# Three of four attention units with scores by rows in place of two of three, and the order of a group's loads

## The chip, the cores and the metric

The kernel runs on one core of one Trainium2 chip. The metric is the device time in microseconds (us); the runs shown agree to the last digit, 1306.41 us. Smaller is better. All times of single instructions come from one execution recorded by the hardware profiler.

## What is computed

The reference is an adaptive layer norm around two blocks; only the first matters here.

```python
h = _layernorm(x, axis=-1) * (1 + ca) + sa
x = x + ga * _A_ref(h, A_k_cache, A_v_cache, A_wq, A_wo)     # attention
h = _layernorm(x, axis=-1) * (1 + cb) + sb
x = x + gb * _B_ref(h, B_w_in, B_w_sp, B_b_sp, B_w_out)      # gated MLP with a mix over positions

# _A_ref: 2048 queries, 2048 cached keys, 32 query heads of width 128 on 8 key/value heads
q = (x @ wq)...; scores = q k^T / sqrt(128); p = softmax(scores); o = p v; return o @ wo
```

Everything is bf16. Each of the 8 key/value heads serves a group of four query heads.

## The kernel before

**Units.** Attention is cut into `NU` = 128 units, numbered `u`: 8 groups (one key/value head each) by 16 tiles of 128 queries, all four query heads of the group in one unit. A unit has 8 slots. In iteration `it` the main loop issues, slot by slot, the scores of unit `it` (`qk`, L1016), the product with V of an earlier unit (`pv_part`, L1449), a quarter of the next block's Q projection (`fill`), and the output projection W_o of a still earlier unit (`wo_proj`, L1156). TensorE runs this in the order in which it is written; nothing is rescheduled.

**Two ways to compute a unit.** Both need 16 score matmuls of 128x512 and 8 exponentials of 128x1024 on ScalarE.

- *Without rows* (I call it a column unit): the scores come out transposed, keys on partitions (L1068), the exponential (L1075) is written straight into the unit's `pT` tile, and the product with V (L1124) takes 64 matmuls of 128x129, the extra column being the sum of the row. VectorE normalises (`onorm`, L1135/L1136), one DMA transpose of 128 KB on SP's queue turns `onorm` into `oT` (L1147), and the four heads of W_o add up in one PSUM bank, followed by one addition (L1168).
- *By rows* (a row unit): the scores have queries on partitions (L1031), the exponential (L1038) also sums its row, and writes into one of six row buffers `pn` (`win_sb` in three parts, `wmod_a`, and two tiles `pn`). When a head's two halves are done, one DMA transpose of 128x2048, 512 KB, on SP's queue carries it into the unit's `pT` tile (`turn_rows`, L1085, the DMA on L1088). The product with V (L1103) then takes 16 matmuls of 128x512 and gives `oT` directly. In exchange each head of W_o has its own bank and its own scaled addition on VectorE (L1174).

Each of the first matmuls with V of a row unit reads all four heads' columns of `pT`, so it needs all four transposes of the unit to have landed.

**Which unit is which, and when its product with V runs.** `by_rows` (L992) says yes for units from `TURN_A` = 5 up to `TURN_B` by a repeating pattern as long as `LAGS`, all of whose entries but the last are row units. `pv_at` (L997) puts the product with V as many units later as the entry says; column units have 1. With `LAGS = (2, 3, 1)` a period is: row (two units later), row (three later), column (one later). That makes 78 row units and 50 column units. `wo_at` is three units after that. Three homes for `pT` (`pT0`, `pT1`, and the tile `wsp`) are handed out in rotation.

**SP's queue** runs in the order in which it is written: the transposes of a row unit's heads one after another, the `onorm` transpose of a column unit behind the first row unit that follows it, and the loads. A column unit has no row transposes of its own.

**Loads.** Each group needs W_q, K (a DMA transpose from memory), V and W_o, 512 KB each, loaded during the group before (L1347 to L1362). Each is placed into slot 1 of the first column unit that comes at least `from_it` units after the start of the group before, one load in one column unit. All of it has two buffers. W_q of a group is first used four units before the group starts, K in its first unit, V one unit later, W_o four units later.

Of the kernel before, what the change touches and what calls it, by code (L numbers as in the profile page):

```python
# [575 lines left out]
def kernel(  # L576
# [19 lines left out]
    nc = tc.nc  # L596
# [13 lines left out]
    CT = 512 // P  # L610
# [107 lines left out]
    def load_wq(g, engine):  # L718
        wqs[g] = early.tile([P, NDT, REP * DH], BF16, name="wq_g")
        engine.dma_start(  # L720
            out=wqs[g][:], in_=wq_dram[:, :, g * REP * DH : (g + 1) * REP * DH]
        )

    def load_v(g):
        v1 = late.tile([P, NKT, DV], BF16, name="v1")
        nc.gpsimd.memset(v1[:, :, DH:DV], 1.0)
        if g > 0:
            nc.sync.dma_start(out=v1[:, :, 0:DH], in_=v_dram[:, g])
        else:
            nc.sync.dma_start(out=v1[:, 0 : NKT // 2, 0:DH], in_=v_rows)  # L730
            nc.sync.dma_start(
                out=v1[:, NKT // 2 : NKT, 0:DH], in_=v_dram[:, 0, NKT // 2 : NKT]
            )
        groups.setdefault(g, {})["v1"] = v1

    def load_wo(g, engine):
        wo_g = late.tile([P, REP, D], BF16, name="wo_g")
        engine.dma_start(out=wo_g[:], in_=wo_dram[:, g * REP : (g + 1) * REP, :])
        groups[g]["wo"] = wo_g

    def load_k(g):
        kT = early.tile([P, SK], BF16, name="kT")
        nc.sync.dma_start_transpose(out=kT[:], in_=A_k_cache[0, g])
        groups.setdefault(g, {})["kT"] = kT
# [240 lines left out]
    NU = HKV * NT  # L985


    TURN_A, TURN_B = CT + 1, NU - 6

    LAGS = (2, 3, 1)  # L990

    def by_rows(u):  # L992
        return TURN_A <= u < TURN_B and (u - TURN_A) % len(LAGS) < len(LAGS) - 1

    row_units = [u for u in range(NU) if by_rows(u)]

    def pv_at(u):  # L997
        return u + (LAGS[(u - TURN_A) % len(LAGS)] if by_rows(u) else 1)

# [13 lines left out]
    def at(it, slot, fn):  # L1013
        later.setdefault((it, slot), []).append(fn)
# [332 lines left out]
    for g in range(1, HKV):  # L1347
        it = (g - 1) * NT
        loads = (
            (0, lambda g=g: load_wq(g, nc.sync)),  # L1350
            (4, lambda g=g: load_v(g)),
            (6, lambda g=g: load_wo(g, nc.sync)),
            (8, lambda g=g: load_k(g)),
        )
        last = it - 1
        for from_it, load in loads:
            if g == 1 and from_it < 6:
                at(3, 3, load)
                continue
            last = next(u for u in pauses if u >= it + from_it and u > last)  # L1360
            at(last + 1, 1, load)
# [316 lines left out]
```

## Time and profile before

| | |
|---|---|
| time, median and both runs | 1306.41 us |
| the profiled execution's own time | 1306.41 us |
| its span, first to last instruction | 1304.6 us |
| mean granted TensorE clock | 0.999 |
| VectorE busy | 684.1 us (52%) |
| exponential of 128x1024 (L1038, L1075) | 1.024 us each |
| `onorm` transposes, L1147 | 50, median 1.295 us on SP's queue |
| one head's scaled addition, L1174 | 0.748 us |
| column unit's one addition, L1168 | 0.679 us |
| `oT` copy of a row unit, L1112 | 0.69 us |
| `tot` and its reciprocal, L1092/L1095 | 0.155 and 0.164 us |
| reciprocal and `onorm`, L1135/L1136 | 0.17 and 0.424 us |

How to read it: "busy" on TensorE counts matmuls from start to modelled end, and these overlap, so the distance between starts is the better measure of what a matmul costs. A line of the timeline gives the start in us from the first instruction, the length, the engine, the source line, the operation, what it writes and reads, and the number merged. `SPq` marks a DMA issued from SP's queue: the length is the time that SP spent on the issue, not the time until the data landed. The list of DMA issues gives that second time, in us from the start of the issue.

### The profile page before, as it was taken

What the parts mean: (1) busy time and instruction counts of PE and PEld (TensorE: products, weight loads), DVE (VectorE), ACT (ScalarE), POOL (GpSimd) and SP (SyncE); (2) the same over time, 40 slices, a digit from 0 to 9 for tenths busy, and PEclk for the clock granted to TensorE, in tenths of its full rate; (3) what the DMA queues carried; (4) which work ended last, traced back from release to release, by engine and by line L of the source; (5) the groups of instructions that cost most, each with busy time, mean ns of one, the idle gap of its engine ahead of it and who ended that gap; (6) DMA issues with size and microseconds to landing.
All of it is one profiled execution on the core that took longest, in us unless ns stands there. A gap on an engine that the chain in (4) does not pass through costs nothing.

```text
span 1304.6 us, 22478 instructions
## 1 busy us (share of the span) xinstructions
PE 1287.9 (99%) x8472; PEld 698.1 (54%) x8626; DVE 684.1 (52%) x1772; ACT 1113.4 (85%) x1683; POOL 57.4 (4%) x93
## 2 busy tenths in 40 slices
PE   8999999999999999999999999999999999999998
PEld 6655555555555555555555555555555556644445
DVE  5635445544554455445544554455445566784443
ACT  7999999999999999999999999999999998650000
POOL 1000000000000000000000000000000133410000
PEclk9999999999999999999999999999999999999999
DMA  7899899999999999999999999999999983264300
GB/s 187 183 198 189 157 190 182 190 170 189 181 194 168 188 173 184 183 181 183 185 188 173 183 187 189 172 185 176 177 198 163 168 151 90 49 137 98 81 21 31
DMA packets 774982, 211.19 MB, mean 162 GB/s; under 512 B 759248, under 2 KB 773200, under 8 KB 774864
## 3 DMA queue, kind: packets, MB, share of 16 engines
q1 hardware_dynamic: 772416, 207.55, 87.0%
q10 hardware_dynamic: 2448, 2.10, 0.5%
q8 instruction: 70, 1.15, 0.4%
q14 instruction: 48, 0.39, 0.1%
HBM read 21.37 MB, written 2.10 MB: 18 GB/s over the span
## 4 chain that ended last, share of the span: by engine, by line
PE 95%; DVE 2%; ACT 1%; DMA 1%; issue 1%; POOL 0%; SPq 0%; ACTq 0%
PE s_ps L1031 21%; PE o_ps L1103 20%; PE o_ps L1124 14%; PE s_ps L1068 13%; PE misc L1181 8%; PE misc L967 8%; PE misc L1545 7%; PE o_ps L1578 1%; PE s_ps L1411 1%; PE s_ps L1372 1%; DVE stz L1394 1%; PE s_ps L1578 0%; DMA wmod_a<-in_w_mod_dram 0%; ACT pT L1075 0%; DMA xnT<-xn 0%
## 5 line engine op out<-in xcount | busy, mean ns | idle before, releaser
L1031 PE MATMUL s_ps<-kT,qT 128*128 128x512 bf16 x1219 | 364.9, 379 | 2.3
L1038 ACT ACTIVATE win_sb<-s_ps 128x1024 bf16<-128x1024 f32 x312 | 319.2, 1024 | 3.8 <-PE s_ps L1031 0.7
L1103 PE MATMUL o_ps<-pT,v 128*128 128x512 bf16 x909 | 272.5, 379 | 1.3
L1174 DVE SCALAR_TENSOR_TENSOR xacc<-misc,rall,xacc 128x512 f32<-128x512 f32 x304 | 227.4, 748 | 68.2 <-PE misc L1181 60.7
L1068 PE MATMUL s_ps<-qT,kT 128*128 128x512 bf16 x784 | 233.2, 379 | 1.9 <-ACT pT L1075 1.1
L1075 ACT ACTIVATE pT<-s_ps 128x1024 bf16<-128x1024 f32 x216 | 217.8, 1025 | 12.9 <-PE s_ps L1068 4.9
L1038 ACT ACTIVATE pn<-s_ps 128x1024 bf16<-128x1024 f32 x208 | 213.0, 1024 | 2.0 <-PE s_ps L1031 0.5
L1103 PEld LDWEIGHTS <-v 128*128 128x128 bf16 x1248 | 122.1, 98 | 147.3
L1075 ACT ACTIVATE wsp<-s_ps 128x1024 bf16<-128x1024 f32 x176 | 179.9, 1024 | 12.1 <-PE s_ps L1068 4.2
L1181 PE MATMUL misc<-wo_g,oT 128*128 128x512 bf16 x479 | 181.5, 379 | 1.0
L967 PE MATMUL misc<-hT,wq_g 128*128 128x512 bf16 (+2 forms) x499 | 179.6, 370 | 0.5
L1031 PEld LDWEIGHTS <-qT 128*128 128x128 bf16 x1248 | 121.5, 98 | 109.4 <-issue 0.4
L978 DVE CAST qT<-misc 128x512 bf16<-128x512 f32 x127 | 87.2, 687 | 151.2 <-PE misc L967 151.2
L1124 PEld LDWEIGHTS <-pT 128*128 128x128 bf16 x1792 | 119.6, 98 | 50.5
L1092 DVE TENSOR_TENSOR tot<-rs 128x1 f32<-128x1 f32 x312 | 48.4, 155 | 171.5 <-ACT win_sb L1038 115.2
L1124 PE MATMUL o_ps<-v,pT 128*128 128x129 bf16 x1792 | 137.5, 220 | 0.6
L1068 PEld LDWEIGHTS <-kT 128*128 128x128 bf16 x784 | 75.6, 98 | 83.0 <-DVE qT L978 1.5
L1124 PEld LDWEIGHTS <-wsp 128*128 128x128 bf16 x1408 | 94.3, 98 | 41.5
L1124 PE MATMUL o_ps<-v,wsp 128*128 128x129 bf16 x1408 | 108.5, 220 | 0.5
L1038 ACT ACTIVATE wmod_a<-s_ps 128x1024 bf16<-128x1024 f32 x104 | 106.4, 1024 | 0.4 <-PE s_ps L1031 0.4
L1545 PE MATMUL misc<-wsp,z 128*128 128x512 bf16 (+2 forms) x554 | 100.1, 336 | 0.4
L1103 PE MATMUL o_ps<-wsp,v 128*128 128x512 bf16 x292 | 87.8, 379 | 0.4
(111 smaller groups left out, 874.3 us busy)
## 6 DMA issues: line engine op xcount, KB each, us to landing
wo_g<-in_A_wo_dram SPq DMA_DIRECT2D x8, 512.0 KB, 5.0
wq_g<-in_A_wq_dram SPq DMA_DIRECT2D x7, 512.0 KB, 4.0
v<-in_A_v_cache_dram SPq DMA_DIRECT2D x7, 512.0 KB, 4.5
wsp<-in_w_mod_dram SPq DMA_DIRECT2D x1, 2048.0 KB, 8.7
out_dram<-yout ACTq DMA_DIRECT2D x16, 128.0 KB, 1.7
pT<-win_sb SPq DMA_TRANSPOSE x117, 4.8
win_sb<-in_B_w_in_dram SPq DMA_DIRECT2D x1, 1792.0 KB, 8.0
x_sb<-in_A_x_dram SPq DMA_DIRECT2D x3, 512.0 KB, 7.0
```

The lines of the kernel that those rows point to most:

```text
L967: nc.tensor.matmul(ps[0][:, o0 : o0 + n], lhsT=wqs[g][:, dt, hh * DH : (hh + 1) * DH], rhs=hTs[ch][:, dt, c0 : c0 + n], start=(dt == 0), s ...
L978: nc.vector.tensor_copy(out=dst, in_=src)
L1031: nc.tensor.matmul(s_ps[:, c * 512 : (c + 1) * 512], lhsT=qTs[b][:, hh, jj * P : (jj + 1) * P], rhs=groups[g]["kT"][:, k0 : k0 + 512], sta ...
L1038: nc.scalar.activation(out=rows_of(u, hh)[:, half * HK : (half + 1) * HK], in_=s_ps[:], func=ACT.Exp, scale=inv_sqrt_dh, accum_out=rsums[u ...
L1068: nc.tensor.matmul(s_ps[:, h * 512 : (h + 1) * 512].rearrange("p (r q) -> p r q", r=REP), lhsT=groups[g]["kT"][:, kt * P : (kt + 1) * P], ...
L1075: nc.scalar.activation(out=pTs[u][:, 2 * i : 2 * i + 2, :], in_=s_ps[:].rearrange("p (k q) -> p k q", k=2), func=ACT.Exp, scale=inv_sqrt_dh,)
L1092: nc.vector.tensor_tensor(out=tot[:], in0=rs[:, 2 * hh : 2 * hh + 1], in1=rs[:, 2 * hh + 1 : 2 * hh + 2], op=ALU.add)
L1103: nc.tensor.matmul(o_pss[u][:], lhsT=groups[g]["v1"][:, kt, 0:DH], rhs=pTs[u][:, kt, :], start=(kt == 0), stop=(kt == NKT - 1),)
L1124: nc.tensor.matmul(o_ps[:, hh % 2, 0 : DH + 1], lhsT=pTs[u][:, kt, hh * P : (hh + 1) * P], rhs=groups[g]["v1"][:, kt, 0 : DH + 1], start=( ...
L1174: nc.vector.scalar_tensor_tensor(out=xa[:], in0=X_ps[:], scalar=scale, in1=xa[:], op0=ALU.mult, op1=ALU.add)
L1181: nc.tensor.matmul(ps[0][:], lhsT=oTs[u][:, hh, :], rhs=groups[g]["wo"][:, hh, :], start=(hh == 0 or each), stop=(hh == REP - 1 or each),)
L1545: nc.tensor.matmul(g_pss[f][:, :n], lhsT=z2[:, st, f * P : (f + 1) * P], rhs=wsp[t][:, st, c0 : c0 + n], start=(st == 0), stop=(st == NT - ...
```

## The change

`LAGS` becomes `(2, 2, 3, 1)`: the period is row, row, row, column, and the products with V run two, two, three and one units later. `TURN_B` moves from `NU - 6` to `NU - 7`, so that units 5 to 120 are 29 whole periods. Row units go from 78 to 87, column units from 50 to 41. All column units of the pattern are now multiples of four, four in each group of 16. The order of the loads becomes W_q, K, V, W_o, so that in the steady state the four column units 4, 8, 12 and 16 units after the start of the group before carry one each. In the first group, W_q and V go out together in unit 3 as before.

```diff
-    TURN_A, TURN_B = CT + 1, NU - 6
-
-    LAGS = (2, 3, 1)
+    TURN_A, TURN_B = CT + 1, NU - 7
+
+    LAGS = (2, 2, 3, 1)
...
             (0, lambda g=g: load_wq(g, nc.sync)),
-            (4, lambda g=g: load_v(g)),
-            (6, lambda g=g: load_wo(g, nc.sync)),
-            (8, lambda g=g: load_k(g)),
+            (4, lambda g=g: load_k(g)),
+            (6, lambda g=g: load_v(g)),
+            (8, lambda g=g: load_wo(g, nc.sync)),
         )
         last = it - 1
         for from_it, load in loads:
-            if g == 1 and from_it < 6:
+            if g == 1 and from_it in (0, 6):
                 at(3, 3, load)
                 continue
```

## The prediction

> **What bounds the kernel now.** I read the page first. TensorE is busy for nearly the whole span, and SP's queue (q1) keeps the DMA engines busy for most of it:
>
> ```profile
> span 1304.6 us, 22478 instructions
> PE 1287.9 (99%) x8472; PEld 698.1 (54%) x8626; DVE 684.1 (52%) x1772; ACT 1113.4 (85%) x1683; POOL 57.4 (4%) x93
> ...
> q1 hardware_dynamic: 772416, 207.55, 87.0%
> ```
>
> Next, the list of waits for TensorE alone. It has five lines, 3.1 us in all. The longest two are below; none names a row transpose. So today every `pT` is there in time, and the end is set by TensorE's own work.
>
> ```profile
> PE o_ps L777 <- DVE onorm L768: 1.2, 1, 1.2
> PE s_ps L1068 <- ACT pT L1075: 1.1, 1, 1.1
> ```
>
> Third, TensorE's timeline over one period: units 56 (row), 57 (row), 58 (column), and the row unit 59 after them. The lines are the first score matmuls of 57, of 58, of 59 and of 60; right after 59's first scores comes 58's product with V.
>
> ```profile
> 503.20 0.59 PE L1031 MATMUL s_ps<-kT,qT 128*128 128x512 bf16 x2
> ...
> 511.84 0.59 PE L1068 MATMUL s_ps<-qT,kT 128*128 128x512 bf16 x2
> ...
> 520.47 0.59 PE L1031 MATMUL s_ps<-kT,qT 128*128 128x512 bf16 x2
> 520.90 0.62 PE L1124 MATMUL o_ps<-v,pT 128*128 128x129 bf16 x8
> ...
> 529.28 0.59 PE L1031 MATMUL s_ps<-kT,qT 128*128 128x512 bf16 x2
> ```
>
> Units 57 and 58 take 8.64 and 8.63 us, whether their scores are by rows or not, because both run a row unit's product with V. Unit 59, which runs a column unit's product, takes 529.28 - 520.47 = 8.81 us. That 0.18 us is all TensorE saves per unit turned to rows.
>
> Fourth, SP's queue over the same period, then the last row transpose of unit 57 by itself (it is the second of the merged pair before the load) with its time to landing, and the range over all 312 row transposes.
>
> ```profile
> 497.27 4.49 SPq L1088 DMA_TRANSPOSE pT<-pn  x2
> 501.86 5.09 SPq L1088 DMA_TRANSPOSE pT<-win_sb  x2
> 507.04 1.28 SPq L1147 DMA_TRANSPOSE oT<-onorm  x1
> 508.41 3.22 SPq L1088 DMA_TRANSPOSE wsp<-win_sb  x1
> 511.72 2.68 SPq L1088 DMA_TRANSPOSE wsp<-wmod_a  x1
> 514.50 4.67 SPq L1088 DMA_TRANSPOSE wsp<-pn  x2
> 519.22 0.74 SPq L738 DMA_DIRECT2D wo_g<-in_A_wo_dram  x1
> ```
>
> ```profile
> 516.69 2.48 SPq L1088 DMA_TRANSPOSE wsp<-pn  x1
> wsp<-pn SPq DMA_TRANSPOSE x1, 4.6
> ```
>
> ```profile
> DMA to landing us min/median/max: 4.2/4.7/7.1
> ```
>
> SP goes from one transpose to the next with no pause, and falls behind. Heads become ready every 2.16 to 2.2 us (two slots); the eight transposes of this period land at 501.67, 504.09, 506.67, 509.08, then (after the `onorm` one) 513.78, 516.13, 518.98 and 521.30. That is 19.63 us for seven transposes and one `onorm` transpose of about 1.25 us: a pace of 2.63 us. Today the column unit lets the queue empty, and unit 57's product is due three units after its start, at about 529.7: 8.4 us to spare.
>
> **TensorE's gain.** Nine units turn to rows: 9 x 0.18 = 1.6 us less. Nothing else on TensorE changes in number: 16 score matmuls and four of W_o per unit both ways.
>
> **The second row unit's shorter lag.** In the new period (r0, r1, r2, column) r1's product moves from three units later to two. Its first matmul with V then stands where 520.90 stands above, 25.87 us after the first exponential of r0 (495.03). The eighth landing, 521.30, misses that by 0.40 us. I worked this out for all 39 periods of the trace, each from its own rows: the eighth landing comes 25.63 us after the pair's start at the earliest, 26.12, 26.40 and 26.97 at the quartiles, 30.37 at the latest (the last pair, whose queue also carries transposes of the second layer norm); 36 of 39 miss 25.87, and the mean of what is missing is 0.84 us. Where TensorE waits for a DMA in the prologue (L874, L1052), it starts 0.04 us after the landing, so I take 0.89. TensorE has no slack in which to recover this (99% busy), so each such wait goes into the total.
>
> **The queue's longer run.** Four more transposes follow in each period. From a mean landing of 26.6 they end at 26.6 + 4 x 2.63 = 37.1; a load adds 2.2 us (loads land 1.3 to 3.9 us behind the transpose before them), so 39.4 us after r0's start. The period is three units of 8.63 and one of 8.81: 34.70, with the wait 35.6. So the queue ends 3.8 us into the next period, while its first head lands at 6.7 at the earliest: a load that ends by about 4.4 costs nothing. Where today's loads ended 4.1 to 5.6 us into a period, the first landing came 0.0 to 0.65 us later than 6.65. With the scatter of both I take 0.15 us per period. Bounds for the two together: 0 (landings at the pace of the plain loads, below) and 1.8 us (pace 2.73), from which I take 1.04, as the eighth landings of 39 periods are the nearest row.
>
> **The sum.** 29 periods x 1.04 = 30.2; less 1.6. The profiled execution took 1306.4 us, 1304.6 of it span, and equals the median: 1306.4 + 30.2 - 1.6 = 1335.0 us.
>
> **What costs nothing, and its cover.** r0 keeps two units: its fourth transpose lands 14.66 us after its start (median, at most 16.69), due at 17.2. r2 has three units; its last landing, 37.1, is due at 43.3. The row buffers go round every six heads: r2's last head starts to write at 23.9, and the sixth transpose must have read by then; it lands at 21.3. That slack of 2.6 us is what is late next, and then ScalarE stalls first. VectorE gets four scaled additions, four sums and reciprocals and a copy for two normalisations and one addition: 4.96 for 1.87 us, 28 us in all, beside 684 busy of 1304.6; without that cover 28 us. ScalarE needs no longer for a row unit than for a column unit (both 8.63). The `onorm` transpose keeps its place behind r0's four; nine fewer (1.25 us each) and 36 more row transposes (2.63 each) are counted in the periods. The loads are 26 in column units as today; with the new order K, V and W_o of a group are issued 8, 5 and 4 units (69, 43, 34 us) before use and land in 5 us; uncovered, one would cost some 5 us per group, 35 in all. The two products in one iteration near the end (unit 123, 12.2 us) move to 122 unchanged.
>
> **Rivals.** *No wait at all.* If transposes went at the pace at which plain loads follow in the same queue (2.2 us), the eighth would land at 6.65 + 7 x 2.2 + 1.25 = 23.3, 2.6 us early, and only the gain would be left: 1306.4 - 1.6 = 1304.8. It decides from a pace of 2.56 us down. For it: single steps of 2.4 occur, and SP's issue alone takes under that. Against: 36 of 39 periods. I give it 0.15. [...]
>
> *The DMA engines become the bound.* One period's DMA work is 12 p + 1.25 + 2.4 us at a pace of p. At 2.63 it is 35.2, below the 35.7 of a period with its wait; from p = 2.68 on it is the longer, and then the queue never empties. At 2.8, as in the slower steps (2.79 is the mean of the fifth to sixth landing), it is 37.25: 2.55 us per period, 29 x 2.55 - 1.6 = 72, 1379 us. For it: by the view by windows the DMA share is 1.01 from 460 to 560 us already, and the next period asks for 6.95 MB in 34.7 us, 200 GB/s, where that window moved 182. Against: such steps are followed by short ones. I give it 0.20 for all beyond 1356 or close to it.
>
> That the change doesn't do what it says is out: built, its SP queue has twelve row transposes and one load per period.
>
> **Chances and range.** My forecast has 0.65, and within it 1332.5, which is 2% above 1306.4 and about what a measurement can tell from no change, lies a little below the middle: 0.27 of 0.65 under it. Same: 0.15 + 0.27 = 0.42; slower 0.38 + 0.20, less the 0.01 that I leave to faster, as no term here gives 26 us: 0.57. The range runs from the no-wait case, 1304, to 1356 (p = 2.73 or 1.8 us per period). The forecast's own range is 1320 to 1350.
>
> **What would show it.** TensorE's waits: a new line for L1103 behind a row transpose, some 25 to 29 times, about 1 us each, 30 us in all, in column units. Column units' starts to the next 9.5 to 9.7 us apart, all others 8.63 or 8.81. SP's queue without pause in the column unit. Wrong if L1103 waits for nothing (the first rival), if ScalarE's L1038 waits for row buffers or the DMA rate stays at 200 GB/s with waits of 2 us and more (the second), or if W_o, V or K are waited for.

## The result and the profile after

The changed kernel takes 1339.59 us (two runs, 1339.19 and 1339.99) where the kernel before takes 1306.41: a ratio of 1.0253, 95% interval 1.0235 to 1.0271. It is slower, by 33.2 us. The profiled execution has a span of 1337.3 us, 32.7 more than before.

From the page of the changed kernel: the span, the busy times, and the chain that ended last, by engine and by line.

```profile
span 1337.3 us, 21946 instructions
PE 1301.5 (97%) x8194; PEld 677.9 (51%) x8194; DVE 705.3 (53%) x1844; ACT 1115.5 (83%) x1755; POOL 57.5 (4%) x93
...
q1 hardware_dynamic: 842400, 225.25, 92.4%
...
PE 87%; DMA 10%; ACT 1%; issue 0%; DVE 0%; SPq 0%; ACTq 0%
PE s_ps L1031 19%; PE o_ps L1103 19%; PE o_ps L1124 11%; DMA pT<-win_sb 10%; PE s_ps L1068 9%; PE misc L967 8%; PE misc L1545 7%; PE misc L1181 7%; PE s_ps L1372 2%; PE s_ps L1411 2%; PE o_ps L1578 1%; ACT pn L1038 1%; PE s_ps L1578 0%; ACT pT L1075 0%; DMA wmod_a<-in_w_mod_dram 0%
```

In the kernel before, the same line of the chain by engine reads:

```profile
PE 95%; DVE 2%; ACT 1%; DMA 1%; issue 1%; POOL 0%; SPq 0%; ACTq 0%
```

So a row transpose, `pT<-win_sb`, now stands in the chain, which ran through TensorE almost alone before. (Its 10% are whole times from issue to landing, some 4.9 us each, not what was lost.) TensorE's list of waits says who waits for it (waiting instruction, releaser, us in all, times, longest):

```profile
PE o_ps L1103 <- DMA pT<-win_sb: 24.0, 24, 3.0
PE o_ps L1103 <- issue: 2.1, 1, 2.1
PE o_ps L777 <- DVE onorm L768: 1.2, 1, 1.2
PE s_ps L1068 <- ACT pT L1075: 1.1, 1, 1.1
...
PE o_ps L1103 <- DMA pT<-wmod_a: 0.4, 1, 0.4
```

The first line is new, and so are the second and the last: the row units' product with V waits for its transposes. (A gap is counted from the modelled end of the matmul before, which lies some 0.17 us behind the start that the next one could have had: the matmul at 367.12 below is 0.38 us long and the next starts 0.21 us after it, so each line is a little less than what was lost.) One such wait in detail, in column unit 40 of the period that starts with unit 37: TensorE's timeline, then the chain of waits over the same stretch (start, us, what).

```profile
365.35 0.59 PE L1068 MATMUL s_ps<-qT,kT 128*128 128x512 bf16 x2
366.69 0.59 PE L1103 MATMUL o_ps<-pT,v 128*128 128x512 bf16 x2 [0.74 <-DMA pT<-win_sb]
367.12 0.38 PE L967 MATMUL misc<-hT,wq_g 128*128 128x512 bf16 x1
367.33 0.59 PE L1068 MATMUL s_ps<-qT,kT 128*128 128x512 bf16 x2
```

```profile
361.68 4.87 DMA pT<-win_sb
366.55 0.14 issue
366.69 0.59 PE o_ps L1103 x2
```

The product would have started at 365.35 + 0.43 = 365.78. The last transpose of unit 38 (the second of the three row units) was issued at 361.68 and landed at 366.55; TensorE goes on 0.14 us later, 0.91 late, and unit 40 lasts 9.54 us in place of 8.63. The row units keep their 8.63 us, or 8.81 behind a column unit, within 0.3 us at the two ends. The one exception is unit 119, which is 0.6 us too long: the last line of the list above, the product of the last period's first row unit.

Over the 29 periods the column units exceed 8.63 us by 34.2 us in all. With the 0.6 us of unit 119, and less the 2.0 us that TensorE saves where nothing waits (the first experiment below), that is 32.8, which accounts for the 32.7. The 25 in the middle exceed 8.63 us by 20.9 us, 0.84 each. Units 8, 12, 116 and 120 exceed it by 2.20, 3.93, 3.96 and 3.21: 13.3 us together.

In two of those four, 12 and 116, the wait is not all. Unit 12 waits 2.08 us and is 3.93 us too long. (The view names no releaser there, but the last transpose lands 0.09 us before the product starts.) TensorE's timeline shows longer matmuls after the wait, and the view by windows (engines' busy time in the order PE, PEld, DVE, ACT, POOL, then granted clock, DMA share, GB/s) a lower clock:

```profile
116.52 0.95 PE L1103 MATMUL o_ps<-pT,v 128*128 128x512 bf16 x2 [2.08 <-issue]
117.26 0.63 PE L967 MATMUL misc<-hT,wq_g 128*128 128x512 bf16 x1
...
120.79 0.38 PE L967 MATMUL misc<-hT,wq_g 128*128 128x512 bf16 x1
```

```profile
116.40:120.70 4.30, 4.18 (x12) 1.64 (x13) 0.00 (x0) 1.17 (x2) 0.00 (x0) 0.60 1.02 201
120.70:127.00 6.30, 6.30 (x33) 2.91 (x31) 1.30 (x3) 6.00 (x6) 0.00 (x0) 1.00 1.04 201
```

The clock record has two such stretches inside the kernel, from 116.61 and from 1045.04 us, each 3.41 us at 0.5. (A third, from 1335.17 us, stands at the kernel's end; the kernel before has one there too.) That is 2 x 1.7 = 3.4 of the 13.3 us. So of the 34.2 us, 30.8 are waits and 3.4 the lower clock.

### The profile page after: what moved, and what is told of

Same layout as the page of the kernel before. It is cut to its first block, busy times and chain, and to the rows that moved or that the text cites. A ratio compares the mean times of both kernels' runs of the same rounds, so it can differ in the third digit from the quotient of the medians.

```text
span 1337.3 us, 21946 instructions
## 1 busy us (share of the span) xinstructions
PE 1301.5 (97%) x8194; PEld 677.9 (51%) x8194; DVE 705.3 (53%) x1844; ACT 1115.5 (83%) x1755; POOL 57.5 (4%) x93
## 4 chain that ended last, share of the span: by engine, by line
PE 87%; DMA 10%; ACT 1%; issue 0%; DVE 0%; SPq 0%; ACTq 0%
PE s_ps L1031 19%; PE o_ps L1103 19%; PE o_ps L1124 11%; DMA pT<-win_sb 10%; PE s_ps L1068 9%; PE misc L967 8%; PE misc L1545 7%; PE misc L1181 7%; PE s_ps L1372 2%; PE s_ps L1411 2%; PE o_ps L1578 1%; ACT pn L1038 1%; PE s_ps L1578 0%; ACT pT L1075 0%; DMA wmod_a<-in_w_mod_dram 0%
## 5 line engine op out<-in xcount | busy, mean ns | idle before, releaser
L1031 PE MATMUL s_ps<-kT,qT 128*128 128x512 bf16 x1392 | 414.0, 379 | 0.1
L1038 ACT ACTIVATE win_sb<-s_ps 128x1024 bf16<-128x1024 f32 x348 | 355.9, 1024 | 5.0 <-PE s_ps L1031 1.1
L1075 ACT ACTIVATE pT<-s_ps 128x1024 bf16<-128x1024 f32 x304 | 308.3, 1025 | 55.4 <-PE s_ps L1068 44.8
L1103 PE MATMUL o_ps<-pT,v 128*128 128x512 bf16 x928 | 277.8, 381 | 26.6 <-DMA pT<-win_sb 24.0
L1103 PEld LDWEIGHTS <-v 128*128 128x128 bf16 x1392 | 134.3, 98 | 198.5 <-issue 34.3
L1124 PEld LDWEIGHTS <-pT 128*128 128x128 bf16 x2496 | 166.8, 98 | 71.8
L1068 PE MATMUL s_ps<-qT,kT 128*128 128x512 bf16 x640 | 191.4, 381 | 1.1 <-ACT pT L1075 1.1
L1124 PE MATMUL o_ps<-v,pT 128*128 128x129 bf16 x2496 | 191.7, 220 | 0.0
L1103 PE MATMUL o_ps<-wsp,v 128*128 128x512 bf16 x464 | 137.3, 379 | 0.0
L1112 DVE CAST oT<-o_ps 128x512 bf16<-128x512 f32 x87 | 60.2, 692 | 96.4 <-PE o_ps L1103 90.2
L1545 PEld LDWEIGHTS <-z 128*128 128x128 bf16 x560 | 50.5, 98 | 48.4 <-issue 0.2
L967 PEld LDWEIGHTS <-wq_g 128*128 128x128 bf16 x528 | 50.7, 98 | 43.6 <-issue 1.0
```

What stands on the lines that cost most here:

```text
L967: nc.tensor.matmul(ps[0][:, o0 : o0 + n], lhsT=wqs[g][:, dt, hh * DH : (hh + 1) * DH], rhs=hTs[ch][:, dt, c0 : c0 + n], start=(dt == 0), s ...
L1031: nc.tensor.matmul(s_ps[:, c * 512 : (c + 1) * 512], lhsT=qTs[b][:, hh, jj * P : (jj + 1) * P], rhs=groups[g]["kT"][:, k0 : k0 + 512], sta ...
L1038: nc.scalar.activation(out=rows_of(u, hh)[:, half * HK : (half + 1) * HK], in_=s_ps[:], func=ACT.Exp, scale=inv_sqrt_dh, accum_out=rsums[u ...
L1068: nc.tensor.matmul(s_ps[:, h * 512 : (h + 1) * 512].rearrange("p (r q) -> p r q", r=REP), lhsT=groups[g]["kT"][:, kt * P : (kt + 1) * P], ...
L1075: nc.scalar.activation(out=pTs[u][:, 2 * i : 2 * i + 2, :], in_=s_ps[:].rearrange("p (k q) -> p k q", k=2), func=ACT.Exp, scale=inv_sqrt_dh,)
L1103: nc.tensor.matmul(o_pss[u][:], lhsT=groups[g]["v1"][:, kt, 0:DH], rhs=pTs[u][:, kt, :], start=(kt == 0), stop=(kt == NKT - 1),)
```

## The experiments

The theory: the second row unit's product (r1) is due two units on, before its last transpose lands (the deadline). The rival: the DMA engines have more work than a period holds (throughput). Each run also has runs of the kernel before on the same chip beside it; their medians lie between 1306.07 and 1306.79.

**One transpose less, of the second or of the third row unit.** Both save the same DMA work; only the first moves the deadline. The diff is that of the second row unit; for the third, the 1 is a 2.

```diff
+                if (u - TURN_A) % len(LAGS) == 1:
+                    nc.gpsimd.memset(pTs[u][:, :, (REP - 1) * P : REP * P], 0.0)
...
-        nc.sync.dma_start_transpose(
-            out=pTs[u][:, :, hh * P : (hh + 1) * P], in_=rows_of(u, hh)
-        )
+        if hh < REP - 1 or (u - TURN_A) % len(LAGS) != 1:
+            nc.sync.dma_start_transpose(
+                out=pTs[u][:, :, hh * P : (hh + 1) * P], in_=rows_of(u, hh)
+            )
```

> The changed kernel, but the fourth head's transpose of every second row unit (r1) is left out; GpSimd sets those columns to zero at the unit's start instead. Deadline theory (r1's last transpose lands after its product is due, two units on): what counts is now the seventh landing, 24.1 us (median of the changed kernel) after the period's start, due at 25.87, so nearly all waits of L1103 go: 1304 to 1308 us. Throughput theory (the DMA engines have more than a period's work in a period): 11 x 2.63 + 1.25 + 2.4 = 32.6 us of work in 34.7, so the waits go as well: 1304 to 1308.

> The same saving of one transpose per period, but of the third row unit (r2), whose product has three units; those columns are set to zero by GpSimd. Deadline theory: r1's eighth transpose is as late as ever, only what the queue carries into the next period shrinks; 25 waits of about 0.7 us and the four long ones at the two ends, 1322 to 1338 us. Throughput theory: same DMA work as with the second unit's transpose left out, so the same time, 1304 to 1308.

Measured: 1304.78 us without r1's fourth transpose, 1330.32 without r2's; before, 1306.79. The first list of TensorE's waits has no DMA in it; its longest line is below. The second still has L1103 (here on line 1106):

```profile
PE o_ps L777 <- DVE onorm L768: 1.2, 1, 1.2
```

```profile
PE o_ps L1106 <- DMA pT<-win_sb: 15.2, 20, 2.2
```

The same bytes saved in two places differ by 25.5 us, of which 3.4 are again the lower clock, which the second run shows twice. So what counts first is r1's last transpose, not the sum of the work. The first run also shows TensorE's gain alone: 2.0 us below the kernel before, forecast 1.6. Each of these two times, like the next two, is a single run.

**No loads.** The changed kernel without the loads of groups 1 to 7. Shown for K; W_q, V and W_o go the same way.

```diff
     def load_k(g):
+        if g > 0:
+            groups.setdefault(g, {})["kT"] = groups[0]["kT"]
+            return
         kT = early.tile([P, SK], BF16, name="kT")
```

> The changed kernel without the 28 loads of groups 1 to 7: every group uses the W_q, K, V and W_o of group 0. Deadline theory: the loads stand behind r1 in the queue, so only what is carried into the next period goes (0.15 us each, and part of the long wait in unit 12): 1326 to 1336 us. Throughput theory: 12 x 2.63 + 1.25 = 32.8 us of work in 34.7, no waits: 1304 to 1308.

Measured: 1327.18 us. The deadline alone, with loads out of the way, costs 1327.2 - 1304.8 = 22.4 us, 0.77 per period. The loads add 12.4 us, more than the 4.4 us and a part of one long wait that the expectation gave them. Of this, 3.4 is the lower clock, which this run does not show before its end; the other 9.0 are 0.31 per period. This does not measure the 0.15 of the prediction: that was to be added to landings of the kernel before, which have loads among them already. From r1's eighth landings, the mean of what is missing is 0.66 us here, 0.84 in the kernel before and 0.95 in the changed kernel.

**The order of the loads alone**, on the kernel before.

```diff
-            (4, lambda g=g: load_v(g)),
-            (6, lambda g=g: load_wo(g, nc.sync)),
-            (8, lambda g=g: load_k(g)),
+            (4, lambda g=g: load_k(g)),
+            (6, lambda g=g: load_v(g)),
+            (8, lambda g=g: load_wo(g, nc.sync)),
...
-            if g == 1 and from_it < 6:
+            if g == 1 and from_it in (0, 6):
```

> The kernel before with only the loads' order changed (W_q, K, V, W_o), the units and lags as before. Both theories: nothing is waited for, 1306.4 us within 1 us. A third, that the order itself costs (K or V late, or a load in the way of a row transpose), would show some of the 33 us here.

Measured: 1306.12 us beside 1306.79. The order costs nothing. The reverse, the new periods with the old order, wasn't tried: K would be loaded in slot 1 of its group's first unit, which reads it in slot 0.

**A later product.** In the column units TensorE's work is put in another order, with nothing left out: first what needs no transpose, then the product with V. In the shorter shift W_o's matmuls (`wf`) stand behind the product instead.

```diff
...
+        todo = []
+        if TURN_A < it < TURN_B and not by_rows(it) and len(pvs) == 1 and by_rows(pvs[0]):
+            for i in range(NSLOT):
+                todo += fill.pop((it, i), [])
+            todo += wf
+            todo += [lambda kt=kt, u=pvs[0]: pv_rows(u, 0, 1, [kt]) for kt in range(NKT)]
+            pvs, wf = [], []
+        per = len(todo) / NSLOT
         for i in range(NSLOT):
...
+            for fn in todo[round(i * per) : round((i + 1) * per)]:
+                fn()
```

> The changed kernel, all of its work; in column units of the pattern the Q projection's and W_o's eight matmuls are issued first, three per slot, so r1's product with V starts 2.6 us later in TensorE's order. Deadline theory: of the eighth landings of the changed kernel only one misses its time by over 2.6 us (2.87): 0.3 us of waits are left, with something for what the queue no longer gains by the waits: 1305 to 1309 us, at or a little below the kernel before. Throughput theory (35.2 us of DMA work in 34.7): the lag would build up until the waits are back at 0.5 us per period: 1316 to 1320.

> As the run with the later product, but only the four matmuls of the Q projection go first: the product with V starts 1.3 us later than in the changed kernel. Deadline theory: the parts of the misses beyond 1.3 us, 5.0 us in all, remain: 1308 to 1313 us. Throughput theory: 1316 to 1322, as with the longer shift.

Measured: 1314.97 us with 2.6 us (five runs, 1311.91 to 1316.3; ratio to the kernel before 1.0068, interval 1.0054 to 1.0082), 1321.22 with 1.3 us (one run). Most of the loss is back, but neither theory had both numbers: the second lies in the throughput theory's range, the first between the two ranges. Most of TensorE's waits are gone with the longer shift (first line, on line 1104; the trace is of the fastest of the five runs), and a new wait of ScalarE has come (second line, from ScalarE's waits): a row buffer whose transpose has not been read yet.

```profile
PE o_ps L1104 <- DMA pT<-win_sb: 2.5, 6, 0.8
```

```profile
ACT pn L1038 <- DMA pT<-pn: 1.2, 2, 0.9
```

The landings say why. The first landing of a period comes (median, after its start) 6.69 us in the kernel before, 6.82 in the changed one, 7.74 with the shorter and 8.15 with the longer shift; the eighth at 26.40, 26.65, 27.54 and 28.03. With fewer waits the queue gets less time to empty, and its lag grows until something waits again. So the throughput limit lies right behind the deadline.

**Both out of the way, and a control.**

> The later product (Q projection and W_o first in column units) together with no loads for groups 1 to 7, which all use group 0's W_q, K, V and W_o. Open is whether the 9 us by which the later product alone stays above the kernel before come from a queue that has more work than a period holds. If so (both theories hold, one behind the other): 12 x 2.62 + 1.25 = 32.7 us of work in 34.7, the first landing of a period back from 8.15 to 6.7 us, and no waits but one or two near the ends: 1304.5 to 1307 us. If the shift itself costs something (TensorE's order, the PSUM banks), it stays at 1310 or more.

> The kernel before (two of three by rows, its own lags and loads), with the same shift of the product with V in its column units. No transpose is late there, so if the shift costs nothing by itself: 1306 us within 1. If it does, more than that, by the same 7 to 9 us that are open.

Measured: the longer shift without loads takes 1305.97 us (1305.80 to 1306.32; ratio 0.9997, interval 0.9988 to 1.0007), and no `pT` is waited for. So the 9 us that were left were the queue's. The shift itself costs next to nothing there: TensorE has one new wait, 1.2 us for a bank, in unit 121 just behind the last shifted unit. The control went the other way, 1358.5 us, and says nothing of that: in the kernel before, W_o in a column unit belongs to a row unit, with a PSUM bank and a scaled addition for each head. Three of them in a slot wait for banks (line 1182 here), twice in nearly every column unit:

```profile
PE misc L1182 <- DVE qT L978: 21.5, 38, 0.6
PE misc L1182 <- DVE xacc L1175: 18.2, 38, 0.5
```

In the changed kernel's column units W_o belongs to a column unit, with one bank for four heads, and there they may be packed: the one bank wait above, 1.2 us, comes behind the last of them.

**Periods of three and of two in turn.** With seven lags the queue can empty, by an estimate from the trace's 2.62 us per row transpose, 1.25 per `onorm` transpose and 2.4 per load: 59.1 us of DMA work in 60.8. Four runs: without the shift, with it in all column units, with it only where W_o belongs to a column unit (the last line of the diff), and so turned that two row units stand at both ends.

```diff
-    LAGS = (2, 2, 3, 1)
+    LAGS = (2, 2, 3, 1, 2, 3, 1)
...
-        return TURN_A <= u < TURN_B and (u - TURN_A) % len(LAGS) < len(LAGS) - 1
+        return TURN_A <= u < TURN_B and LAGS[(u - TURN_A) % len(LAGS)] > 1
...
+        if TURN_A < it < TURN_B and not by_rows(it) and len(pvs) == 1 and by_rows(pvs[0]) and not any(by_rows(u) for u in wos):
```

```diff
-    TURN_A, TURN_B = CT + 1, NU - 7
+    TURN_A, TURN_B = CT + 1, NU - 8
...
-    LAGS = (2, 2, 3, 1, 2, 3, 1)
+    LAGS = (2, 3, 1, 2, 2, 3, 1)
```

> The same mixed periods without the later product. DMA work of seven units is 59.1 us in 60.8, so the queue empties. Throughput theory alone: no waits, 1304.5 to 1307.5. Deadline theory: each of the 17 periods of three still waits 0.7 to 0.9 us, with long ones at the ends: 1317 to 1326.

> The whole work, with periods of three and of two row units in turn (lags 2, 2, 3, 1, 2, 3, 1), 83 row units, and the later product in column units. Seven units hold 20 x 2.62 + 2 x 1.25 + 1.75 x 2.4 = 59.1 us of DMA work in 60.8 us, so the queue can empty; TensorE saves 5 x 0.18 = 0.9 us against the kernel before. If both theories are right, 1304.5 to 1307.5 us, with one or two waits at the ends. If the deadline alone counted, the same; if any period of three costs its wait whatever the queue holds, 16 x 0.3 = 5 us more.

> Periods of three and of two row units in turn, with the later product only in the column units behind three row units; the others keep their order, since there W_o belongs to a row unit, whose four scaled additions can't come faster than one per slot (the 33 us of bank waits in the mixed run before). The queue can empty and the product is late enough: both theories give 1306.4 - 0.9 = 1305.5, between 1304.5 and 1307.5 with a wait or two at the ends.

> The mixed periods with the later product, but turned so that the first and the last period have two row units (lags 2, 3, 1, 2, 2, 3, 1 up to unit 119; 82 row units). The one long wait of the mixed run, 1.3 us in unit 11, should go, as no period of three follows the prologue. Both theories: 1306.4 - 4 x 0.18 = 1305.7, between 1305.0 and 1306.5, at or just below the kernel before. If it stays at 1307 or above, the mixed run's remainder is not in the ends.

Measured: without the shift 1320.92 us (ratio 1.0107, interval 1.0092 to 1.0123); its list of waits has L1103 behind transposes for some 10 us:

```profile
PE o_ps L1103 <- DMA pT<-win_sb: 4.1, 5, 1.8
PE o_ps L1103 <- DMA wsp<-wmod_a: 3.1, 3, 2.0
PE o_ps L1103 <- DMA pT<-pn: 3.0, 3, 1.5
```

So a period of three waits although the queue empties before it: its first landing is back at 6.65 us (median), and still the eighth misses 25.87 us in all 17 periods of three. Their 17 column units are 15.3 us too long together, 0.90 each; the column units behind periods of two keep 8.63 us. Less 0.9 us of gain, that is the 14.4 us more than the kernel before. That is the deadline by itself again.

With the shift in every column unit it is 1327.4, well above what was expected: the bank waits of the control again (two lines like those above, 9.0 and 7.7 us in 32 waits, some 22 us with the 0.17 that each is counted short, and not the 33 that the expectation of the next run names), and none for a transpose.

With the shift only where W_o belongs to a column unit 1307.01 (ratio 1.0006, interval 0.9997 to 1.0015), with one wait for a transpose left, 1.3 us in unit 11. With two row units in the first and the last period 1305.71 us, as forecast to the tenth: eleven runs from 1305.32 to 1305.87, beside fifteen of the kernel before from 1306.0 to 1306.65, and no transpose is waited for in its trace. The ratio, 0.9995, has an interval of 0.9986 to 1.0004, so whether it beats the kernel before is not settled by that; it does all of the work and beats the changed kernel by 34 us.

## Why the prediction was right

**The sum.** Forecast 1335.0 us, measured 1339.2 in the profiled execution (median 1339.6). By terms: waits in column units 30.8 us, forecast 30.2; the wait in unit 119 0.6, forecast none; the lower clock 3.4, not in the sum; TensorE's gain 2.0, forecast 1.6. These add up to the difference of 4.2. So the mechanism and its size were right, and what was missing was the clock above all.

**The bound and TensorE's gain.** As forecast: 8.81 us for a unit that runs a column unit's product, 8.63 for all others, and 2.0 us of gain where nothing waits (1.6 forecast).

**The deadline.** The step that carried the forecast holds. The eighth landing came at 26.65 us (median) for a due time of 25.87, and missed it in 27 of 29 periods. Taking r1's last transpose away removes the loss, taking one of r2's away leaves most of it. The wait by itself is 0.77 us per period without loads; I had 0.89 from the kernel before, loads included.

**The queue's carry and the start.** The waits are 1.06 us per period, where I had 1.04. Of that, the mean miss of the eighth landing is 0.95, so the queue's longer run added 0.11 to the 0.84 of the kernel before; I had 0.15. TensorE's start behind the landing adds the other 0.11: it starts 0.13 us behind in most periods, 0.05 in the others, where I took 0.05 from the prologue. The two small errors went against each other.

**The middle and the ends.** The prediction used one mean over 39 periods, and 29 periods have the same four at the two ends. In the kernel before these four miss by 1.18, 2.06, 2.42 and 4.50 us, and the other 35 by 0.65 on average. In the changed kernel the four ends wait 2.2, 2.2, 2.3 and 3.2 us, 9.9 together, and the 25 in the middle 0.84 each. That the one mean came out right is in part luck: the same trace taken by its parts, with 0.05 and 0.15 added to each period, gives 25 x 0.85 + 10.2 + 4 x 0.2, some 32 us, an estimate.

**What was not in the sum.** The clock fell to half after two of the long waits, 3.4 us; no term of mine had a price for a wait beyond its own length. And r0's cover, 17.2 us for a fourth landing of at most 16.69, failed once: in the last period it landed at 17.71, and unit 119 was 0.6 us longer.

**The pace.** 2.62 us per row transpose (19.62 us for seven and one `onorm` transpose, mean of 23 periods in the middle; 2.63 forecast); r2's last landing at 37.3 us (37.1). The rival without waits, which decides from 2.56 us down, fell with that. 512 KB in 2.62 us is 200 GB/s.

**The throughput rival.** It is not what bounds the changed kernel, as the pair of shortened runs shows, but I had set it too far off: as soon as the deadline is moved, it takes 9 us back. Two of the prediction's figures on this side are slightly off: the mean of the fifth to the sixth landing is 2.84 us over all 39 periods, not 2.79, and a pace of 2.73 gives 1.71 us per period by its formula, not 1.8. Neither is in the sum; the second would lower the range's upper end by 2 us.

**What was to cost nothing.** The order of the loads cost nothing (1306.12 beside 1306.79). No load of the groups 1 to 7 was waited for. VectorE's busy time rose by 21 us (28 forecast) without holding up TensorE. The row buffers were not late in the changed kernel, and were what was late next, as forecast, once the product had been put later. My assumption in the control, that W_o may be moved together with the Q projection, was wrong for row units (1358.5 us).

## What to carry to other kernels

When a change shortens the time between a transfer and its use, take the landing times of the same transfer from the trace of before and hold them against the new due time, period by period; the mean of the misses was most of the forecast here (0.84 of 1.04 us per period), and it was there to be read before the change was made. Take the ends of the loop by themselves where they differ. A full queue and a short deadline look alike in a profile: saving the same bytes once in front of the deadline and once behind it tells them apart (1304.78 and 1330.32 us here). And a wait that can't be removed can be filled, by putting the work that needs no transfer first in the unit, provided that this work has its own banks free (1314.97 us in place of 1339.59 where it had, 1358.5 in place of 1306.4 where it had not).

## What the hardware showed that I had not expected

After some waits of about two microseconds TensorE's clock fell to half. In the changed kernel a wait of 2.08 and one of 2.11 us were followed by 3.41 us at a granted clock of 0.5, but one of 2.03 and one of 3.05 us were not; in the run with r2's transpose left out, waits of 1.96 and 2.20 us were, and one of 2.57 us in the run without loads was not. So the length of the wait alone does not decide it; what does was not tried.
